# Bilinear FFN behind block-sparse attention: sampled value blocks gathered by GpSimd's indirect DMA, other transfer times in the planner, no parking of products

## Chip, cores and metric

The kernel runs on one core of a Trainium2 chip. The metric is the device time of one execution in microseconds; the time given for a kernel is the median of its runs.

## What is computed

Four batches of eight heads attend over 768 positions of 64 elements, in blocks of 32 positions. The first and the last block attend to everything and are attended by everything, each other block sees its two neighbours and three sampled blocks, which are an input. The result, 3072 rows of 512, goes through a feed-forward layer without a nonlinearity but the product of two projections.

```python
mask = np.abs(blk_i - blk_j) <= window
mask = mask | (blk_i == 0) | (blk_j == 0) | (blk_i == n_blocks - 1) | (blk_j == n_blocks - 1)
for qb in range(n_blocks):
    for kb in sampled_blocks[qb]:
        mask[qb*block:(qb+1)*block, kb*block:(kb+1)*block] = True
...
attn = attn / (np.sum(attn, axis=-1, keepdims=True) + 1e-09)
out = np.matmul(attn, v)                       # then x = out as (B*S, H*D)
a = x @ w_a; b = x @ w_b                       # 512 -> 1536
return a * b @ w_out                           # 1536 -> 512
```

## The kernel before

Work goes by **units**: one query block of 32 positions with all eight heads, 96 in all. Eight units make a **chunk** of 256 positions; there are 12 chunks, three to a batch. Of the 24 units of a batch 22 are sparse (`attend`), the first and the last are dense (`attend_all`).

A sparse unit runs like this. GpSimd (POOL) copies its eight key blocks into `KG`, one of two buffers (`gather_keys`, L573 to L578; the three sampled blocks by addresses that it loads into registers, L553). TensorE (PE) makes the scores `s` (L873, L772), VectorE (DVE) their maximum, ScalarE (ACT) the exponentials `sm`, and the two of them a high and a low half of the weights `hl` (L790 to L797). A transposing DMA on the queue of SyncE (SP) turns `hl` into `pt` (L920). PE multiplies `pt` by the unit's value blocks in `VG` (`av`, L816). `VG` also has two buffers; a unit's eight blocks come from `vd`, the values in DRAM, by DMAs of SP (`gather_values`): the three neighbours in one (L608), the first and last block where the buffer does not hold them yet (L610, L611), and each sampled block by a DMA of its own, whose address SP reads from the table `offs` into a register (L553, L613). A buffer is free when `av` of the unit two before it has run. Two units make a stretch of `xT`, the input of the feed-forward layer (L1060, L1063).

The feed-forward layer runs by chunk and by twelve slices f of the 1536 inner columns: `first_products` makes a and b (`ab`, 24 matmuls, L1098), `inner` multiplies them (L1126, L1129), `split` makes two float32r parts `gh` and `gl` (L1153, L1156), `second_products` multiplies them by `w_out` (`o`, six matmuls, L1184 to L1186). The weights arrive as 64-bit words in 36 loads of 512 KB, and DVE and ACT turn each into the parts that PE reads (L709 to L753); a chunk's slice f waits for `w_ready[f]` in the first chunk. With `PARK` set the second chunk is a flow of its own: `inner` stores its twelve products `a` to DRAM (`parked_g`, L1134), and `unpark` fetches each again (L1147) before it is split.

The order on every engine is fixed at build time by `Plan`. Each step names an engine, a time that it is thought to take and, for a DMA, the time that its bytes hold the DMA engines; the planner issues the step that it thinks can begin first. On the chip every engine works its list off in order, so a step that waits holds whatever stands behind it, on SP's and POOL's queues too. Every DMA of SP and of ACT also takes the next of eight semaphore lanes, and waits until the DMA that had the lane before has landed.

Of the kernel before, what the change touches and what calls it, by code (L numbers as in the profile page):

```python
# [30 lines left out]
LANDING = 1200  # L31
LANES = 8
# [23 lines left out]
PARK = True  # L56
# [69 lines left out]
class Plan:  # L126
# [13 lines left out]
    def begin(self, flow, way):  # L140
# [103 lines left out]
def kernel(  # L244
# [9 lines left out]
    c_blocks: bass.AP,  # L254
    out: bass.AP,
# [69 lines left out]
    offs = const.tile([1, NB, 4], I32, name="offs")  # L325
# [26 lines left out]
    vg_ready = {u: Event() for u in vg_units}  # L352
# [31 lines left out]
    def make_tables():  # L384
# [3 lines left out]
        row = work.tile([P, DM], F32, tag="st", name="mrow", bufs=ST_BUFS)  # L388
# [6 lines left out]
        one = row[0:1, 0 : 2 * NR * NB].bitcast(I32).rearrange("p (a b) -> p a b", b=2)  # L395
        clamped = row[0:1, 256 : 256 + NR * NB]
        clamped3 = clamped.rearrange("p (a b) -> p a b", b=NR)

        def load():
            nc.scalar.dma_start(  # L400
                one.rearrange("p a b -> p (a b)"),
                sampled_blocks.bitcast(I32).rearrange("(o a) b -> o (a b)", o=1),
            )
            nc.scalar.dma_start(
# [6 lines left out]
        def starts():  # L411
            nc.vector.tensor_scalar(
                clamped, one[:, :, 0], 0.0, float(NB - 1), ALU.max, ALU.min
            )
            nc.vector.tensor_scalar(
                offs[:, :, :NR], clamped3, float(BLK), None, ALU.mult
            )
            nc.vector.tensor_scalar(
                offs_k[:, :, :NR], clamped3, float(BLK // 2), None, ALU.mult
            )  # L420

        t = yield dve(700, starts)
# [46 lines left out]
    def keys(b, g):  # L469
        yield from gate(first_of[b] - GATE_KV)  # L470
        raw, freed = yield from raw_tile(b, g, 0)
        yield load_way(1000, lambda: nc.scalar.dma_start(raw, k[b, g]))
# [23 lines left out]
        end = yield sp(1700, 2200, lambda: nc.sync.dma_start_transpose(  # L496
# [6 lines left out]
    def values(b, g):  # L503
# [3 lines left out]
        yield load_way(1000, lambda: nc.scalar.dma_start(raw, v[b, g]))  # L507
# [42 lines left out]
    def dynamic(engine, table, i):  # L550
        eng = {"SP": mybir.EngineType.SP, "POOL": mybir.EngineType.Pool}[engine]
        step, top = (BLK, S - BLK) if table is offs else (BLK // 2, (S - BLK) // 2)
        return nc.values_load_multi_w_load_instructions(  # L553
            table[0:1, i, :NR], engines=(eng,), min_val=0, max_val=top,
# [3 lines left out]
    def gather_keys(n):  # L558
# [13 lines left out]
        def copies():  # L572
# [4 lines left out]
            for r, at in enumerate(dynamic("POOL", offs_k, i)):  # L577
# [8 lines left out]
    def gather_values(n):  # L586
# [10 lines left out]
        def copies():  # L597
# [14 lines left out]
            for r, at in enumerate(dynamic("SP", offs, i)):  # L612
                nc.sync.dma_start(  # L613
                    to[(1 + r) * BLK : (2 + r) * BLK, 1, :], vd[b][bass.ds(at, BLK), :]
                )

        dense = i in (0, NB - 1)
        t = yield [Way("SP", 475 if dense else 3000 + 1250 * first, copies, 1300, 1)]
        vg_ready[b, i, x].fire(t + LATE_VG)

# [6 lines left out]
    def queries(cc):  # L627
# [6 lines left out]
        yield load_way(1400, lambda: nc.scalar.dma_start(t[:D], q[b, c]))  # L634
# [36 lines left out]
    def turn_queries(cc, a):  # L671

        end = yield sp(650, 700, lambda: nc.sync.dma_start(
# [12 lines left out]
    def weights(n):  # L686
# [4 lines left out]
        for m in range(n, n + 1 + both):  # L691
            freed.append((yield from take("w", W_BUFS)))
            yield load_way(1350, lambda m=m: nc.scalar.dma_start(
# [162 lines left out]
    def attend(b, i):  # L856
# [63 lines left out]
        t = yield sp(1300, 1500, lambda: nc.sync.dma_start_transpose(  # L920
# [29 lines left out]
    def attend_quad(b, i, hq, ends):  # L950
# [53 lines left out]
        for x in range(2):  # L1004
# [10 lines left out]
            t = yield sp(1100, 1130, lambda hl=hl, pt=pt: nc.sync.dma_start_transpose(  # L1015
# [56 lines left out]
    parked_g = dram.tile([NF, P, CH], F32, name="parked_g")  # L1072
    g_parked = [Event() for _ in range(NF)]
    split_done = [Event() for _ in range(NF)]
# [4 lines left out]
    def first_products(ccs):  # L1079
        for cc in ccs:  # L1080
# [3 lines left out]
            if cc == 2 and PARK:  # L1084
                yield split_done[NF - 1]
            if cc == 0:
                plan.start(second_products(), R_P2)
            for f in range(NF):
                if cc < 2 and (cc == 0 or PARK):
                    yield w_ready[f]  # L1090
# [19 lines left out]
    def inner(cc, f, ab, read):  # L1110
# [22 lines left out]
        if cc == 1 and PARK:  # L1133
# [157 lines left out]
```

## Time and profile before

| | |
|---|---|
| median of three runs | 901.85 us (900.5 to 905.66) |
| the profiled execution | 901.24 us, of which 899.5 us are the span from the first to the last instruction |
| busy in the span | PE 770.2, DVE 580.0, ACT 464.3, POOL 176.9 us |
| DMA | 145.5 MB; 0.83 to 0.99 of the engines in each 50 us up to 400 us |
| chain that ended last | PE 55%, DMA 14%, DVE 10%, ACT 7%, SP's queue 2% |

PE is busy for most of the span and for nearly all of it after 200 us; before that DVE is. A wait on another engine counts only where one of these two waits in the end.

### The profile page before, as it was taken

How to read it: one execution, taken by the hardware profiler on the slowest of the kernel's cores; microseconds unless marked ns; L12 is line 12 of the kernel's file. 1: busy time of each engine (PE TensorE's matmuls, PEld its weight loads, DVE VectorE, ACT ScalarE, POOL GpSimd, SP SyncE). 2: the span in 40 equal slices, each digit the busy share in tenths (PEclk: the TensorE clock that was granted, in tenths of full speed). 3: DMA queues.
4: the chain of work that ended last, by engine and by line, in shares of the span. 5: the costliest groups of instructions: out<-in, count | busy, mean ns of one | idle time of the engine just before them, and what ended most of it. 6: DMA issues, size and time to landing. Idle time of an engine off the chain costs nothing.

```text
span 899.5 us, 23840 instructions
## 1 busy us (share of the span) xinstructions
PE 770.2 (86%) x9024; PEld 619.3 (69%) x9024; DVE 580.0 (64%) x1533; ACT 464.3 (52%) x1118; POOL 176.9 (20%) x416
## 2 busy tenths in 40 slices
PE   0132499678989999999999899999998999999998
PEld 0022277557768777777777678788776878888886
DVE  3898999986558677665677577645867736342222
ACT  4675576586446566754456468335536424232222
POOL 0652142322003332110132331001322200000000
PEclk9998599899999999999999999999999999999999
DMA  9978999979878699985867999637766516351000
GB/s 228 287 186 218 243 235 252 222 193 206 215 205 181 140 194 210 198 181 136 173 155 170 180 211 206 153 82 159 180 134 155 125 29 153 80 121 27 25 1 24
DMA packets 212221, 145.50 MB, mean 162 GB/s; under 512 B 152841, under 2 KB 180490, under 8 KB 211338
## 3 DMA queue, kind: packets, MB, share of 16 engines
q1 hardware_dynamic: 201280, 106.22, 54.3%
q10 hardware_dynamic: 10826, 37.76, 14.4%
q8 instruction: 71, 1.16, 0.5%
q14 instruction: 44, 0.36, 0.1%
HBM read 87.82 MB, written 14.16 MB: 113 GB/s over the span
## 4 chain that ended last, share of the span: by engine, by line
PE 55%; DMA 14%; DVE 10%; ACT 7%; issue 2%; SPq 2%; ACTq 0%; POOL 0%
PE ab L1098 30%; PE o L1184 6%; PE av L816 5%; DMA pt<-hl 5%; PE o L1186 5%; PE o L1185 5%; DMA q<-in_q_dram 3%; PE s L772 3%; DVE low L888 1%; DVE hl L797 1%; DVE xT L1063 1%; DMA VG<-vd 1%; DVE QT L649 1%; DMA u<-parked_g 1%; ACT sm L898 1%
## 5 line engine op out<-in xcount | busy, mean ns | idle before, releaser
L1098 PE MATMUL ab<-xT,wab 128*128 128x256 f16 x3456 | 404.7, 274 | 12.7 <-ACT xT L1060 6.9
L1098 PEld LDWEIGHTS <-wab 128*128 128x128 f16 x3456 | 329.7, 98 | 78.5 <-issue 37.7
L1129 DVE SCALAR_TENSOR_TENSOR a<-a,rscale,ab 128x256 f32<-128x256 f32 x144 | 68.6, 478 | 112.1 <-ACT a L1126 110.9
L1184 PE MATMUL o<-woh,gh 128*128 128x512 f32 x288 | 127.1, 441 | 6.8 <-ACT gh L1153 6.4
L1126 ACT ACTIVATE a<-ab,f 128x256 f32<-128x256 f32 x144 | 67.5, 468 | 120.3 <-PE ab L1098 114.4
L898 ACT ACTIVATE sm<-s,low,cq 128x256 f32<-128x256 f32 x176 | 97.9, 559 | 58.7 <-DVE low L891 29.4
L816 PE MATMUL av<-pt,VG 128*128 128x64 f16 x2688 | 103.2, 196 | 28.9 <-DMA pt<-hl 14.9
L816 PEld LDWEIGHTS <-VG 128*128 128x128 f16 x2688 | 94.6, 100 | 48.1 <-issue 35.5
L573 POOL COPY KG<-keysT 128x384 int32<-128x384 int32 x88 | 56.9, 647 | 356.5 <-PE s L772 325.9
L797 DVE SCALAR_TENSOR_TENSOR hl<-sm,den,hl 128x256 f16<-128x256 f32 (+1 forms) x208 | 104.3, 510 | 21.4 <-ACT hl L790 18.6
L1186 PE MATMUL o<-woh,gl 128*128 128x512 f32 x288 | 115.2, 400 | 0.5 <-DVE gl L1156 0.5
L1185 PE MATMUL o<-wol,gh 128*128 128x512 f32 x288 | 113.6, 395 | 0.0
L578 POOL COPY KG<-keysT 128x128 int32 x264 | 94.5, 394 | 42.9 <-POOL KG L573 23.2
L1153 ACT CAST gh<-a 128x256 fp32r<-128x256 f32 x132 | 53.1, 403 | 59.2 <-DVE a L1129 58.0
L1156 DVE TENSOR_TENSOR gl<-a,gh 128x256 fp32r<-128x256 f32 x132 | 58.2, 441 | 32.3 <-ACT gh L1153 31.6
L1184 PEld LDWEIGHTS o<-woh,gh 128*128 128x128 f32 x288 | 54.7, 190 | 27.7 <-ACT gh L1153 10.0
L772 PE MATMUL s<-KG,QT 128*32 128x256 f16 x1408 | 58.8, 291 | 16.8 <-DMA QT<-QT 16.6
L873 PE MATMUL s<-mrows,ident 128*32 128x192 bf16 (+1 forms) x352 | 25.6, 280 | 54.7 <-ACT sm L898 27.8
L1063 DVE SCALAR_TENSOR_TENSOR xT<-av,xT 64x256 f16<-64x256 f32 x96 | 40.4, 421 | 44.3 <-ACT xT L1060 43.4
L1186 PEld LDWEIGHTS o<-woh,gl 128*128 128x128 f32 x288 | 54.6, 189 | 16.6 <-DVE gl L1156 4.3
L888 DVE TENSOR_REDUCE low<-s 128x2 f32<-128x512 f32 x88 | 59.9, 682 | 6.4 <-PE s L772 6.1
L772 PEld LDWEIGHTS <-QT 128*32 128x32 f16 x1664 | 43.7, 101 | 29.5 <-issue 24.1
(92 smaller groups left out, 736.0 us busy)
## 6 DMA issues: line engine op xcount, KB each, us to landing
VG<-vd SPq DMA_DIRECT2D x284, 64.0 KB, 2.2
VG<-vd SPq DMA_DIRECT2D x88, 192.0 KB, 3.3
VG<-vd SPq DMA_DIRECT2D x32, 384.0 KB, 3.8
q<-in_q_dram ACTq DMA_DIRECT2D x12, 512.0 KB, 6.0
QT<-QT SPq DMA_DIRECT2D x24, 256.0 KB, 3.8
vd<-vs SPq DMA_DIRECT2D x16, 384.0 KB, 4.1
out_dram<-ou SPq DMA_DIRECT2D x24, 256.0 KB, 2.4
stage<-in_k_dram ACTq DMA_DIRECT2D x12, 384.0 KB, 4.2
```

What stands on the lines that cost most here:

```text
L578: nc.gpsimd.tensor_copy(to[:, :, (5 + r) * w : (6 + r) * w], of[:, :, bass.ds(at, w)])
L772: mm(to[h * BLK : (h + 1) * BLK], q_block(cc, i, 4 * hq + h, a), rhs(4 * hq + h), start=(first and a == 0), stop=(a == 1), skip_group_chec ...
L797: t = yield dve(221 + n * 1.03, lambda: nc.vector.scalar_tensor_tensor(lo, sm, over, hi, ALU.mult, ALU.subtract))
L816: mm(av[:, g, i % 2, :], w, pt[:, y, cols], start=(i % 2 == 0 and g == 0 and first and n + m == 0), stop=(last and n == len(terms) - 1 and ...
L888: yield dve(685, lambda: nc.vector.tensor_reduce(mx, ps, axis=mybir.AxisListType.X, op=ALU.max, negate=True))
L898: t = yield act(750, lambda hq=hq: nc.scalar.activation(sm[:, hq], ps[:, hq], AF.Exp, bias=low[:, at, hq, 0:1], scale=cq[:, cc, hq : hq + ...
L1098: mm(ab[:, i, :], wab[:, f, i, part, kt, :], xc[:, kt, a, :], start=(i == 0 and kt == 0 and part + a == 0), stop=(kt == KT - 1 and a == 1) ...
L1126: yield act(470, lambda: nc.scalar.activation(a_sb, ab[:, 0, :], AF.Copy, scale=fb[:, f : f + 1]))
L1129: t = yield dve(420, lambda: nc.vector.scalar_tensor_tensor(a_sb, a_sb, rb, ab[:, 1, :], ALU.mult, ALU.mult))
L1184: mm(po, gh[:, js], woh[:, f, :], start=(f == 0), stop=False)
L1185: mm(po, gh[:, js], wol[:, f, :], start=False, stop=False)
L1186: mm(po, gl[:, js], woh[:, f, :], start=False, stop=(f == NF - 1))
```

## The change

Three edits go together. (1) The three sampled value blocks of a unit come by one indirect DMA issued from POOL (`gather_sampled`): 96 rows, whose row numbers stand in a new table `taken`, one column per block, made at the start from the sampled blocks broadcast to 96 partitions. SP keeps L608, L610 and L611, and no longer reads addresses; the table `offs` is gone. `vg_ready` of a sparse unit now counts two arrivals. (2) `PARK` and all that hangs on it is gone: the second chunk follows the first in one flow. (3) The planner's times for transfers change (loads of keys and values 1000 to 1340 ns, of queries 1400 to 2200, of weights 1350 to 1590, `pt` 1500 to 1650, and so on), and it knows DMAs from POOL, which it books at 1300 ns on POOL and which take no lane of the eight.

```diff
@@ class Plan
-        if way.moved:
+        if way.moved and way.eng != "POOL":
             at = max(at, self.dma - DMA_AHEAD, self.generator)
...
+        if way.moved and way.eng == "POOL":
+            self.free["POOL"] = at + way.ns
+            self.dma = max(self.dma, at + way.ns + GATHER_LATE) + way.moved
+            flow.ready = self.dma + LANDING
+            return
@@ def make_tables
+            for r in range(NR):
+                ps = slice(r * BLK, (r + 1) * BLK)
+                nc.vector.tensor_scalar(
+                    taken[ps], clamped3[ps, :, r], float(BLK), row[ps], ALU.mult, ALU.add
+                )
@@ def gather_values
-            for r, at in enumerate(dynamic("SP", offs, i)):
-                nc.sync.dma_start(
-                    to[(1 + r) * BLK : (2 + r) * BLK, 1, :], vd[b][bass.ds(at, BLK), :]
-                )
...
+        if not dense:
+            plan.start(gather_sampled(b, i, to), order[b, i] - LEAD_G)
...
+    def gather_sampled(b, i, to):
+        t = yield [Way("POOL", 1300, lambda: nc.gpsimd.indirect_dma_start(
+            to[BLK:, 1, :], None, vd[b], bass.IndirectOffsetOnAxis(ap=taken[:, i : i + 1], axis=0),
+        ), 700)]
+        vg_ready[b, i, 0].fire(t + LATE_VG)
@@ def queries
-        yield load_way(1400, lambda: nc.scalar.dma_start(t[:D], q[b, c]))
+        yield load_way(2200, lambda: nc.scalar.dma_start(t[:D], q[b, c]))
@@ def inner
-        if cc == 1 and PARK:
-            t = yield sp(650, 364, lambda: nc.sync.dma_start(parked_g[f], a_sb))
-            e_a.fire(t)
-            g_parked[f].fire(t)
-            return
         yield from split(cc, f, a_sb, e_a)
-
-    def unpark():
-        for f in range(NF):
-            yield g_parked[f]
...
-            t = yield sp(650, 364, lambda f=f: nc.sync.dma_start(a_sb, parked_g[f]))
-            plan.start(split(1, f, a_sb, e_a), R_NOW, t)
@@ end of the kernel
-            plan.start(first_products([0, *range(2, NC)]), R_P1)
-            plan.start(first_products([1]), R_P1 + 1)
+        plan.start(first_products(), R_P1)
```

SP's list shrinks from 976 rows to 337. This is its piece around the first `pt` transposes of batch 0, before; `pt_466`, `pt_587` and `pt_617` belong to units 1, 2 and 3 of the first chunk, and `VG_85` in the first row to its unit 2.

```order
L608 DMA VG_85<-vd_79 96x1024
L553 TENSOR_LOAD offs
L613 ISA
L613 DMA VG_85<-vd_79 32x1024
L613 ISA
L613 DMA VG_85<-vd_79 32x1024
L613 ISA
L613 DMA VG_85<-vd_79 32x1024
L673 DMA QT_440<-QT_440 64x2048
L920 DMA_TRANSPOSE pt_466<-hl_436 128x8x128
L920 DMA_TRANSPOSE pt_587<-hl_513 128x8x128
L920 DMA_TRANSPOSE pt_617<-hl_517 128x8x128
```

And now, from the values of unit 1 on (`pt_415`, `pt_444`, `pt_523` and `pt_602` are units 0 to 3):

```order
L619 DMA VG_86<-vd_79 96x1024
L621 DMA VG_86<-vd_79 32x1024
L622 DMA VG_86<-vd_79 32x1024
L935 DMA_TRANSPOSE pt_415<-hl_364 128x8x128
L935 DMA_TRANSPOSE pt_444<-hl_409 128x8x128
L935 DMA_TRANSPOSE pt_523<-hl_453 128x8x128
L619 DMA VG_85<-vd_79 96x1024
L935 DMA_TRANSPOSE pt_602<-hl_528 128x8x128
```

Units 1 and 2 are turned ahead of the third unit's values, where all of these stood behind them.

On POOL each gather stands between key gathers. This is a place in batch 1, before, where only key copies follow each other (`KG_83` for one unit, then `KG_84` for the next):

```order
L573 COPY KG_83<-keysT_78 128x8x48
L553 TENSOR_LOAD offs_k
L578 ISA
L578 COPY KG_83<-keysT_78 128x8x16
L578 ISA
L578 COPY KG_83<-keysT_78 128x8x16
L578 ISA
L578 COPY KG_83<-keysT_78 128x8x16
L573 COPY KG_84<-keysT_78 128x8x48
```

And now, in the same stretch; the first row brings values for unit 7 of the batch, the copies under it keys for its unit 13:

```order
L631 DMA VG_85<-vd_80,taken 96x1024
L584 COPY KG_83<-keysT_78 128x8x48
L563 TENSOR_LOAD offs_k
L589 ISA
L589 COPY KG_83<-keysT_78 128x8x16
L589 ISA
L589 COPY KG_83<-keysT_78 128x8x16
L589 ISA
L589 COPY KG_83<-keysT_78 128x8x16
L631 DMA VG_86<-vd_80,taken 96x1024
```

The keys of unit 13 stand behind a row that waits until PE has run `av` of unit 5.

On DVE the start is reordered. Before, the first weights (`wab<-stage`) stand ahead of the low half of the first queries (`QT_140`):

```order
L709 TENSOR_SCALAR wab<-stage 128x1024
L488 SCALAR_TENSOR_TENSOR ks_3_144<-wab,scale,ks_3_144 128x12x64
L713 SCALAR_TENSOR_TENSOR wab<-stage,wab 128x1024
L716 SCALAR_TENSOR_TENSOR wab<-stage,wab 128x1024
L649 SCALAR_TENSOR_TENSOR QT_140<-q_109,scale,QT_140 64x2048
```

Now the queries (`QT_150`) and the tables come first, and the first weights 26 rows after the queries:

```order
L500 SCALAR_TENSOR_TENSOR ks_3_138<-wab,scale,ks_3_138 128x12x64
L381 TENSOR_SCALAR power<-power 128x1
L384 TENSOR_SCALAR rscale<-power 128x1
L387 RECIPROCAL scale<-rscale 128x1
L664 SCALAR_TENSOR_TENSOR QT_150<-q_109,scale,QT_150 64x2048
L554 TENSOR_REDUCE bound<-bound_v 128x1
L422 TENSOR_SCALAR mrow<-mrow 96x72
```

The attention of the first chunk moved ahead of the weights on DVE.

## Rows read from the trace of the kernel before

**Rows 1.** The page's first part: busy time, share of the span and instructions of each engine.

```profile
span 899.5 us, 23840 instructions
PE 770.2 (86%) x9024; PEld 619.3 (69%) x9024; DVE 580.0 (64%) x1533; ACT 464.3 (52%) x1118; POOL 176.9 (20%) x416
```

**Rows 2.** Busy time of each engine in stretches of the span, with the granted clock of TensorE (1.00 is its upper level), the share of the DMA engines and what they moved.

```profile
core 0: us, PE busy (x) PEld busy (x) DVE busy (x) ACT busy (x) POOL busy (x), PEclk, DMA share, GB/s
0.00:50.00 50.00, 5.00 (x80) 3.20 (x80) 31.16 (x84) 27.94 (x52) 19.39 (x37) 1.00 0.93 256
50.00:100.00 50.00, 17.36 (x274) 12.64 (x275) 45.07 (x104) 31.88 (x77) 14.34 (x25) 0.85 0.83 211
100.00:150.00 50.00, 39.65 (x489) 31.73 (x487) 46.42 (x115) 32.55 (x78) 17.15 (x33) 0.88 0.99 236
150.00:200.00 50.00, 36.69 (x440) 28.98 (x437) 46.08 (x118) 34.59 (x82) 13.43 (x24) 0.90 0.84 212
200.00:900.00 700.00, 671.49 (x7754) 542.71 (x7751) 411.22 (x1116) 337.30 (x834) 112.64 (x299) 1.00 0.63 142
```

**Rows 3.** What PE waited for between 200 and 900 us: who and line, whom it waited for: us in total, times, longest us.

```profile
PE o L1184 <- ACT gh L1153: 6.4, 7, 2.4
PE av L816 <- DMA pt<-hl: 5.5, 4, 2.6
PE s L873 <- ACT sm L898: 5.3, 6, 1.8
PE av L816 <- DVE xT L1063: 2.5, 4, 1.0
PE av L816 <- DMA VG<-vd: 0.3, 1, 0.3
```

**Rows 4.** The two longest waits of DVE between 50 and 200 us, same columns.

```profile
DVE hl L797 <- ACT hl L790: 4.2, 2, 3.8
DVE power L374 <- POOL power L371: 1.9, 4, 1.1
```

**Rows 5.** The timeline from 54 to 79 us, SP's queue and the engines that wait at its end: start, us, engine, line, operation, count, and in brackets the idle time before it and what ended that.

```profile
54.27 0.47 DVE L797 SCALAR_TENSOR_TENSOR hl<-sm,den,hl 128x256 f16<-128x256 f32 x1
62.87 0.47 DVE L797 SCALAR_TENSOR_TENSOR hl<-sm,den,hl 128x256 f16<-128x256 f32 x1
...
65.83 0.53 SPq L608 DMA_DIRECT2D VG<-vd  x1
68.14 1.32 SPq L613 DMA_DIRECT2D VG<-vd  x3
...
70.08 7.27 SPq L920 DMA_TRANSPOSE pt<-hl  x3
77.71 0.51 ACT L790 ACTIVATE hl<-sm,den 128x256 f16<-128x256 f32 x1 [5.14 <-DMA pt<-hl]
78.25 0.48 DVE L797 SCALAR_TENSOR_TENSOR hl<-sm,den,hl 128x256 f16<-128x256 f32 x1 [3.78 <-ACT hl L790]
```

**Rows 6.** The chain that ended last, from 257 to 265 us, in order of time (start, us, what), and under it PE's row at 262.35 us in the timeline.

```profile
257.05 0.24 PE o L1184
...
258.55 3.26 DMA u<-parked_g
261.89 0.41 ACT gh L1153
...
263.14 0.43 PE o L1185
...
262.35 0.79 PE L1184 MATMUL o<-woh,gh 128*128 128x512 f32 x1 [2.39 <-ACT gh L1153]
```

**Rows 7.** Instructions of SP's queue by line: count, ns minimum/median/maximum, first and last start.

```profile
L553 SPq TENSOR_LOAD <-offs x88: 666/688/1870, 59.1 to 793.8; - x88
L613 SPq DMA_DIRECT2D VG<-vd x264: 315/316/1436, 60.2 to 795.8; - x132
...
L920 SPq DMA_TRANSPOSE pt<-hl x88: 1237/1284/4338, 53.2 to 774.7; - x88
```

**Rows 8.** POOL: its longest wait over the span; its copies of one sampled key block over the span (ns minimum/median/maximum); the same copies grouped from 50 to 200 us and from 200 to 720 us (busy us, mean ns, idle before them); and one unit's keys in the timeline.

```profile
POOL KG L573 <- PE s L772: 325.9, 61, 55.0
...
L578 POOL COPY KG<-keysT x264: 287/293/2775, 32.6 to 716.6; 128x128 int32 x132
...
L578 POOL COPY KG<-keysT 128x128 int32 x48 | 22.6, 506 | 6.6 <-issue 4.5 <-POOL KG L573 2.1
...
L578 POOL COPY KG<-keysT 128x128 int32 x201 | 62.6, 348 | 35.7 <-POOL KG L573 20.5 <-issue 14.0 <-POOL KG L576 1.0
...
705.66 0.51 POOL L573 COPY KG<-keysT 128x384 int32<-128x384 int32 x1 [6.67 <-PE s L772]
707.55 0.82 POOL L578 COPY KG<-keysT 128x128 int32 x3 [1.39 <-issue]
```

**Rows 9.** DVE's groups by shape over the span: busy us, mean ns of one | idle before.

```profile
L488 DVE SCALAR_TENSOR_TENSOR ks<-stage,scale,ks 128x768 f16<-128x768 f32 x12 | 12.1, 1014 | 1.8 <-ACT ks L487 1.7
L747 DVE SCALAR_TENSOR_TENSOR wab<-wab,scale 128x512 f16<-128x512 f32 x16 | 12.0, 759 | 0.8 <-ACT wab L746 0.7
L888 DVE TENSOR_REDUCE low<-s 128x2 f32<-128x512 f32 x88 | 59.9, 682 | 6.4 <-PE s L772 6.1
```

**Rows 10.** Pieces of the chain that ended last with PE at its upper clock: one sparse unit's scores (two rows), one slice of a first product, one unit's `av`.

```profile
121.02 0.20 PE s L873 x4
121.22 0.47 PE s L772 x16
...
223.66 2.62 PE ab L1098 x24
...
245.84 0.71 PE av L816 x24
```

More of the change, by code (lines that the diff above doesn't have):

```diff
@@ L31 @@
 LANDING = 1200
+GATHER_LATE = 600
 LANES = 8
@@ L324 @@
     mrows = const.tile([P, 8, BLK], BF16, name="mrows")
-    offs = const.tile([1, NB, 4], I32, name="offs")
+    taken = const.tile([NR * BLK, NB], I32, name="taken")
+    row = const.tile([NR * BLK, 1], F32, name="row")
     offs_k = const.tile([1, NB, 4], I32, name="offs_k")
@@ L387, in make_tables @@
         held = yield from take("st", ST_BUFS)
-        row = work.tile([P, DM], F32, tag="st", name="mrow", bufs=ST_BUFS)
+        mrow = work.tile([P, DM], F32, tag="st", name="mrow", bufs=ST_BUFS)
         held2 = yield from take("st", ST_BUFS)
@@ L394, in make_tables @@
         dup = box[:NB, 56:64]
-        one = row[0:1, 0 : 2 * NR * NB].bitcast(I32).rearrange("p (a b) -> p a b", b=2)
-        clamped = row[0:1, 256 : 256 + NR * NB]
+        one = mrow[: NR * BLK, 0 : 2 * NR * NB].bitcast(I32).rearrange("p (a b) -> p a b", b=2)
+        clamped = mrow[: NR * BLK, 256 : 256 + NR * NB]
         clamped3 = clamped.rearrange("p (a b) -> p a b", b=NR)
@@ L547, in values_scale, with dynamic @@
         v_scale[b].fire(end)
-    def dynamic(engine, table, i):
-        eng = {"SP": mybir.EngineType.SP, "POOL": mybir.EngineType.Pool}[engine]
-        step, top = (BLK, S - BLK) if table is offs else (BLK // 2, (S - BLK) // 2)
+    def dynamic(i):
         return nc.values_load_multi_w_load_instructions(
-            table[0:1, i, :NR], engines=(eng,), min_val=0, max_val=top,
+            offs_k[0:1, i, :NR], engines=(mybir.EngineType.Pool,), min_val=0,
+            max_val=(S - BLK) // 2,
             skip_runtime_bounds_check_because="the table is clamped to these bounds",
@@ L576, in copies @@
                 nc.gpsimd.tensor_copy(to[:, :, 4 * w : 5 * w], of[:, :, (NB - 1) * w :])
-            for r, at in enumerate(dynamic("POOL", offs_k, i)):
+            for r, at in enumerate(dynamic(i)):
                 nc.gpsimd.tensor_copy(
@@ L1077, with first_products @@
     f1_ready = {(b, f): Event() for b in range(B) for f in range(NF)}
-    def first_products(ccs):
-        for cc in ccs:
+    def first_products():
+        for cc in range(NC):
             b, c = chunks[cc]
@@ L1088, in first_products @@
             for f in range(NF):
-                if cc < 2 and (cc == 0 or PARK):
+                if cc == 0:
                     yield w_ready[f]
@@ L1132, in inner @@
         read.fire(t)
-        if cc == 1 and PARK:
-            t = yield sp(650, 364, lambda: nc.sync.dma_start(parked_g[f], a_sb))
-            e_a.fire(t)
-            g_parked[f].fire(t)
-            return
-        yield from split(cc, f, a_sb, e_a)
-    def unpark():
-        for f in range(NF):
-            yield g_parked[f]
-            if f >= 2:
-                yield split_done[f - 2]
-            e_a = yield from take("a", A_BUFS)
-            a_sb = work.tile([P, CH], F32, tag="a", name=f"u{f}", bufs=A_BUFS)
-            t = yield sp(650, 364, lambda f=f: nc.sync.dma_start(a_sb, parked_g[f]))
-            plan.start(split(1, f, a_sb, e_a), R_NOW, t)
+        yield from split(cc, f, a_sb, e_a)
     def split(cc, f, a_sb, e_a):
@@ L1166, in second_products @@
             b, c = chunks[cc]
-            if cc == 1 and PARK:
-                plan.start(unpark(), R_NOW)
             rows = out[b * S + c * CH : b * S + (c + 1) * CH, :].rearrange(
@@ L1218 @@
         plan.start(attend(*units[0]), 0)
-        if PARK:
-            plan.start(first_products([0, *range(2, NC)]), R_P1)
-            plan.start(first_products([1]), R_P1 + 1)
-        else:
-            plan.start(first_products(range(NC)), R_P1)
+        plan.start(first_products(), R_P1)
         plan.run()
@@ L1236, in _constants @@
     blocks = np.stack([i - 1, i, i + 1, 0 * i, 0 * i + NB - 1], 1)
-    return [("c_blocks", np.concatenate([blocks, np.eye(NB)], 1).astype(np.float32))]
+    rows = np.arange(96)[:, None] % 32
+    return [
+        ("c_blocks", np.concatenate([blocks, np.eye(NB)], 1).astype(np.float32)),
+        ("c_rows", rows.astype(np.float32)),
+    ]
 def _laid_out(name, a):
```

41 lines of the change are left out of this document (17 added, 24 removed).

## Prediction

> **What bounds the kernel now.** I read the page's busy times first, then the stages, then who waits in each. PE is busy for 770.2 of 899.5 us [rows 1], so 129.3 us of idle PE are all that a change which leaves every matmul in place can win, apart from clock. The stages say where they lie [rows 2]: 45.0 us before 50, 56.3 us from 50 to 200, and 28.5 us in the last 700. From 50 to 200 us DVE is busy for 137.6 of 150 us, and ACT for 99.0: DVE, which unpacks the weights beside the attention of the first units, sets the pace there, and PE idles because its work is not ready; its granted clock of 0.85 to 0.90 there costs little for the same reason. After 200 us PE sets the pace, 671.5 of 700 us. So the kernel is a DVE stage and a PE stage, and I ask of each edit what it does to DVE's waits in the first, and to PE's in the second. The DMA engines are 0.83 to 0.99 busy in the first [rows 2], yet DVE waits little for them.
>
> Of PE's idle time after 200 us the waits with a name are 6.4 us for `gh`, 5.5 for `pt`, 5.3 for the exponentials, 2.5 for `xT`; for `VG` it is 0.3 [rows 3]. So the value blocks themselves are hardly ever late in that stage. What the edit can win lies in what stands behind them on SP.
>
> **SP's queue.** A unit's sampled blocks cost SP one table load and three DMAs: 0.69 + 3 x 0.32 = 1.6 us of instructions, and about 2.7 us from the issue at 65.83 to the start of the first of them plus their own 1.32 [rows 5, 7]; 88 times that is 88 x 1.6 = 141 us at least. It goes. The clearest harm is early. The weights `hl` of unit 1 are done at 54.27 + 0.47 us, those of units 2 and 3 by 62.87 + 0.47, but their transposes begin at 70.08, behind the third unit's values [rows 5]. ACT then waits 5.14 us for the buffer and DVE 3.78 us for ACT. In the new order units 1 and 2 stand ahead of those values. I take the 3.8 us off the DVE stage. The bounds are 0, if the transposes themselves are as late in full DMA engines (7.27 us for three, against 1.28 for the median one [rows 5, 7]), and 4.2 us, all that DVE waits for `hl` there [rows 4].
>
> After 200 us the same relief meets the 5.5 us that PE waits for `pt`. Two waits make up most of it, and I halve it: -2.7, between 0 and -5.5.
>
> **The start and DVE's order.** Before the twelfth product of the first chunk (L1129), after which PE is never short of weights again, DVE's new list holds one residual of keys more (1.01 us), one of weights (0.76), one score maximum (0.68), and some small steps, three of them for the new table: by counting the rows ahead of it and multiplying each by its group's mean [rows 9] I get 194.1 us of work against 191.4, so +2.7. The queries and tables now precede the first weights. That brings the first scores nearer, but the same work stands ahead of the twelfth product either way, so I count nothing, with 4 us to either side for what DVE idles while the tables load. The DVE stage: -3.8 + 2.7 = -1.1.
>
> **Parking.** The 24 transfers and their issues go. Their price on PE is one wait: at 262.35 us PE had idled 2.39 us for a `gh` whose product had come back from DRAM in 3.26 us, and the next six matmuls ran at 0.43 us and more where the hot ones take 0.24 [rows 6], the lower of the two clock levels, about 1.3 us. Together -3.7. The other bound is 0: the second chunk's products now go straight from DVE to PE, and another wait for `gh` may stand there.
>
> **PE's own order.** It changes too, and not for the better. Between the end of a slice's `ab` and its first `o` PE's list must hold enough other work to hide two steps of ACT and two of DVE. Adding up matmuls at the hot durations [rows 6, 10], 16 of 144 slices had under 4 us there, now 27 have. The 4.0 us of `gh` waits left besides parking (6.4 - 2.4) [rows 3], spread over 16, make 0.25 us each, so 11 more cost +2.8; the bounds are 0 and +4.4, at 0.4 us each (6.4 over 16).
>
> **Truer transfer times.** Some of the other named waits, those for exponentials and `xT` (7.8 us) [rows 3], come from loads and transposes that took longer than planned. A quarter less is -2; the bounds are -8 and +2.
>
> **The gather on POOL.** The trace has no indirect DMA. Bounds for what one holds POOL: from below 0.29 us, one copied block [rows 8]; from above 4.3 us, the longest transposing issue on SP [rows 7]. The nearest rows are three plain issues for the same 96 rows, 0.95 us, and the median transposing issue, 1.28 us [rows 7]; I take 1.3. POOL has room for it on the whole: 88 x 1.3 = 114 us more, where it idles 325.9 us waiting for PE to free key buffers [rows 8]. But a gather waits for `av` of the unit two before, and the next keys, and the reductions that scale weights and queries, wait behind it. So it matters how much PE work stands between that `av` and the scores which need those keys. At the place shown it is two scores, two `o` slices and one `av`: 2 x (0.20 + 0.47) + 2 x 6 x 0.24 + 0.71 = 4.9 us [rows 6, 10]. This is the least; fourteen units have under 8, 92 us in sum. One unit's keys take 705.66 to 708.37, 2.7 us [rows 8], and about 0.4 us go to semaphores, an estimate. So up to 1.7 us for a gather nothing happens, and 1.3 is free.
>
> **A gather under DVE's pressure.** The row that warns is the key copy: 0.293 us at the median, 0.506 in the mean from 50 to 200 us, where DVE is busy for 92%, and 2.775 at the worst [rows 8]; so work on POOL stretches 1.7 times there, and 1.2 times later (0.348). A gather of 1.3 us would be 2.2 and then 1.5, which stays free after 200 us. The Trainium skill, "SBUF — State Buffer", section "SBUF: two separate sides", goes further: while VectorE holds the port pair it shares with GpSimd, descriptors of a DMA issued from GpSimd cannot be written, and a transfer of 620 ns became 3100 ns beside a VectorE copy. By its fivefold stretch the gather would be 6.5 us, an estimate from that page, and the sum below would rise by some 40 us. The copies' rows agree on the direction and not on the size.
>
> **Sum.** -1.1 (DVE stage) - 2.7 (`pt`) - 3.7 (parking) + 2.8 (PE's order) - 2 (truer times) = -6.7. The span goes from 899.5 to 892.8. The profiled execution took 901.24, 1.74 more, and the median is 0.6 above that, so the median comes to 895.
>
> **The rivals.** *The waits come back (no change).* The second chunk's products wait for `gh` as before, the tight `ab`-to-`o` gaps cost their 4.4 us, and truer times bring nothing: -1.1 - 2.7 + 4.4 = +0.6, less part of the clock, so 902. For it: PE's waits after 200 us are many and short [rows 3], the mark of a list that always has something tight; against it: the parked wait is one place and is gone.
>
> *POOL becomes the queue that blocks (slower).* With g the length of a gather, a unit loses g + 3.1 minus its lead where that is positive. At g = 4 these losses come to 9 us over the tight units, at g = 5 to 14 x 8.1 - 92 = 21 us, and then the median is 895 + 21 = 916. It outweighs the gains at about g = 3.6. For it: copies stretch on POOL, and four other kinds of work hang on that list. Against it: 1.3 us leaves room even at 1.7 times.
>
> *The relief is larger (much faster).* DVE's waits from 50 to 200 us fall by most of the 6 us named [rows 4] and half of the 28.5 us after 200 goes [rows 2]: -4 + 2.7 - 14 = -15, so 886 and less, to 880.
>
> **How the numbers follow.** Main case 0.42, own range 889 to 897; no change 0.25; POOL blocks 0.18; much faster 0.15. A measurement here can tell about 0.5%, 4.5 us, from no change: under 897.3 is faster, over 906.4 slower. Main and much faster are faster, 0.57; the second is the same, with a little of POOL's mild end, 0.25; 0.18 is slower. The range that leaves out two in ten runs from 881, through the larger relief, to 912, into POOL's case at g of some 4.5 us; the predicted time is the main case's.
>
> **What would show it.** SP's list has no L553 and its transposes begin within 2 to 3 us of their `hl` between 60 and 80 us; DVE's wait of 3.78 us there is gone. No wait for `u`, and PE does not idle 2 us near 260. PE's busy time from 200 us on is over 97% and its idle there 20 to 24 us. The gathers hold POOL for 1 to 2 us, and `s` never waits for `KG`. I am wrong if `s` or DVE waits for POOL by more than 5 us in all, if the DVE stage ends more than 4 us away from 200, or if PE's waits for `gh` after 200 us grow beyond 8 us.

## The result and the profile after

The changed kernel takes 907.93 us (median of 20 runs, 902.54 to 918.85) against 903.25 for the kernel before: ratio 1.0051, interval 1.0029 to 1.0072. It is slower by half a per cent where 0.8 per cent faster was forecast. The profiled execution took 903.19 us, with a span of 901.4. All ratios below are to the kernel before on the same chip; they leave out runs over 1.5% above the fastest of their kernel, so a kernel whose runs scatter can have a median that stands higher than its ratio, and both are given (below, x_G's ratio rests on three of its twelve runs and y_truth's on two of six).

The page after, its busy times, and under it the same stretches as [rows 2] (us of PE, PEld, DVE, ACT and POOL, granted clock, share of the DMA engines, GB/s):

```profile
span 901.4 us, 22960 instructions
PE 775.1 (86%) x9024; PEld 620.7 (69%) x9024; DVE 588.9 (65%) x1544; ACT 461.8 (51%) x1109; POOL 264.7 (29%) x504
...
0.00:50.00 50.00, 5.01 (x80) 3.31 (x81) 28.17 (x77) 26.25 (x49) 13.96 (x30) 1.00 0.84 232
50.00:100.00 50.00, 18.62 (x320) 13.85 (x319) 44.60 (x104) 32.15 (x79) 24.30 (x39) 0.80 0.97 214
100.00:150.00 50.00, 42.23 (x526) 33.08 (x522) 47.93 (x114) 33.30 (x80) 25.61 (x43) 0.93 1.04 256
150.00:200.00 50.00, 31.83 (x300) 23.12 (x301) 44.82 (x121) 32.36 (x72) 18.45 (x24) 0.83 0.78 194
...
200.00:901.40 701.40, 677.36 (x7802) 547.35 (x7801) 423.33 (x1131) 337.71 (x832) 182.35 (x371) 1.00 0.69 139
```

Against [rows 1, 2]: POOL does 88 us more, DVE 9 us. PE idles 45.0 us before 50 as it did, 57.3 from 50 to 200 (56.3), and 24.0 after 200 (28.0 by the same cut at the end). So 3 us of idle time went, and PE's busy time grew by 4.9 for the same matmuls. Part of that is the clock: from 50 to 200 us it was lower in two of the three stretches (0.80, 0.93 and 0.83 against 0.85, 0.88 and 0.90), and it fell once more after 310 us (below).

Where the time went shows best in a running account: time, less the matmul work done by then, every matmul at its duration with the clock at its upper level (24 `ab` 2.62 us, an `o` 0.233, 24 `av` 0.71, as [rows 6, 10]), in us lost so far:

| at us | 120 | 200 | 260 | 280 | 330 | 400 | 500 | 850 |
|---|---|---|---|---|---|---|---|---|
| before | 102 | 122 | 126 | 133 | 134 | 141 | 146 | 165 |
| after | 93 | 125 | 131 | 131 | 140 | 144 | 152 | 169 |
| after, gathers left out (y_none) | 92 | 125 | 131 | 131 | 133 | 137 | 146 | 153 |

After is 9 us ahead at 120 us, 3 behind at 200 and 2 ahead at 280, since before loses 7 us where it unparks its products and after loses none there; then after loses 9 us between 280 and 330. The third line is an experiment, below.

PE's waits after 200 us, as [rows 3], and DVE's longest from 50 to 200, as [rows 4]:

```profile
PE av L831 <- DMA VG<-vd,taken: 5.1, 4, 2.4
PE av L831 <- DVE xT L1078: 3.7, 6, 1.6
PE s L888 <- ACT sm L913: 3.6, 3, 2.1
PE o L1175 <- ACT gh L1148: 3.4, 5, 1.6
PE o L1177 <- DVE gl L1151: 1.5, 2, 1.0
...
DVE power L381 <- POOL power L378: 9.1, 5, 4.5
```

`pt` is gone from the list (5.5 before) and `gh` fell from 6.4 to 3.4; but the values, 0.3 before, now stand first. DVE no longer waits for `hl` (4.2), and waits 9.1 us for POOL's reductions (1.9). This is the place of the 4.5, in timeline rows of POOL, of DVE and, last, of SP:

```profile
50.42 1.09 POOL L631 DMA_INDIRECT VG<-vd,taken  x1 [6.58 <-DVE low L903]
51.82 0.92 POOL L631 DMA_INDIRECT VG<-vd,taken  x1 [0.30 <-issue]
52.75 0.51 POOL L584 COPY KG<-keysT 128x384 int32<-128x384 int32 x1
53.20 0.75 POOL L589 COPY KG<-keysT 128x128 int32 x3
53.94 0.30 POOL L378 PARTITION_ALL_REDUCE power<-bound  x1
...
54.28 0.43 DVE L381 TENSOR_SCALAR power<-power 128x2 int32<-128x2 int32 x1 [4.50 <-POOL power L378]
...
52.39 9.76 SPq L935 DMA_TRANSPOSE pt<-hl  x3
```

The first gather holds POOL's list for 6.58 us, and the reduction for which DVE waits stands behind it. What it waits for is not the DVE row named, but most likely the store of the values that it reads: with a plain DMA in its place (y_plain, below), the trace puts 5.63 us of the same wait down to `vd<-vs`:

```profile
50.55 1.19 POOL L631 DMA_DIRECT2D VG<-vd  x2 [5.63 <-DMA vd<-vs]
```

The three transposes of SP take 9.76 us.

The end of the DVE stage, as the start of the first and the twelfth product on DVE, before (L1129) and after (L1139), and the busy times up to the end of the twelfth:

```profile
118.51 0.48 DVE L1129 SCALAR_TENSOR_TENSOR a<-a,rscale,ab 128x256 f32<-128x256 f32 x1
198.82 0.48 DVE L1129 SCALAR_TENSOR_TENSOR a<-a,rscale,ab 128x256 f32<-128x256 f32 x1
...
0.00:199.30 199.30, 98.06 (x1266) 75.97 (x1267) 168.04 (x418) 126.26 (x283) 64.30 (x117) 0.91 0.90 229
```

```profile
108.69 0.48 DVE L1139 SCALAR_TENSOR_TENSOR a<-a,rscale,ab 128x256 f32<-128x256 f32 x1 [0.61 <-ACT a L1136]
205.47 0.47 DVE L1139 SCALAR_TENSOR_TENSOR a<-a,rscale,ab 128x256 f32<-128x256 f32 x1
...
0.00:205.90 205.90, 102.38 (x1296) 76.77 (x1297) 171.19 (x425) 128.77 (x290) 85.32 (x140) 0.88 0.92 223
```

The first product comes 9.8 us earlier and the twelfth 6.6 us later: DVE is busy 3.2 us longer by then and idle 3.4 us longer (34.7 against 31.3). Of the idle time 3.0 us more lie before 50 us (21.8 against 18.8), ahead of the first gather.

The gathers themselves: their time on POOL (ns minimum/median/maximum), two pieces of the chain that ended last, and PE's rows where two of them were late:

```profile
L631 POOL DMA_INDIRECT VG<-vd,taken x88: 918/948/2441, 50.4 to 796.1; - x88
...
91.96 9.12 DMA VG<-vd,taken
...
301.26 9.73 DMA VG<-vd,taken
...
304.86 0.79 PE L831 MATMUL av<-pt,VG 128*128 128x64 f16 x21 [1.55 <-DMA VG<-vd,taken]
311.04 0.79 PE L831 MATMUL av<-pt,VG 128*128 128x64 f16 x21 [2.35 <-DMA VG<-vd,taken]
```

A gather is short on POOL, 0.95 us, but its data are late. From the packets of its queue in the trace (64 to a gather, in order): the first starts 2.8 us after the gather does, the last ends 4.9 us after it at the median and 10.7 at the worst. Before, a 64 KB value block on SP landed 2.2 us after its issue by the page.

### The profile page after: what moved, and what is told of

It is laid out like the page before. It is cut to its first block, busy times and chain, and to the rows that moved or that the text cites. A ratio compares the mean times of both kernels' runs of the same rounds, so it can differ in the third digit from the quotient of the medians.

```text
span 901.4 us, 22960 instructions
## 1 busy us (share of the span) xinstructions
PE 775.1 (86%) x9024; PEld 620.7 (69%) x9024; DVE 588.9 (65%) x1544; ACT 461.8 (51%) x1109; POOL 264.7 (29%) x504
## 3 DMA queue, kind: packets, MB, share of 16 engines
q0 software_dynamic: 5632, 17.31, 9.1%
## 4 chain that ended last, share of the span: by engine, by line
PE 63%; DVE 14%; DMA 11%; ACT 5%; issue 5%; POOL 2%; POOLq 1%; ACTq 0%; SPq 0%; DVEq 0%
PE ab L1108 34%; PE o L1175 6%; PE av L831 6%; PE o L1177 6%; PE o L1176 5%; PE s L787 4%; DMA VG<-vd,taken 3%; DMA stage<-in_k_dram 2%; DMA pt<-hl 2%; DVE hl L812 2%; DVE xT L1078 1%; DMA keysT<-ks 1%; DVE low L903 1%; PE s L888 1%; DVE QT L664 1%
## 5 line engine op out<-in xcount | busy, mean ns | idle before, releaser
L1108 PE MATMUL ab<-xT,wab 128*128 128x256 f16 x3456 | 409.9, 276 | 11.2 <-ACT wab L761 5.4
L631 POOL DMA_INDIRECT VG<-vd,taken x88 | 93.1, 1058 | 302.9 <-PE av L831 271.8
L1139 DVE SCALAR_TENSOR_TENSOR a<-a,rscale,ab 128x256 f32<-128x256 f32 x144 | 68.7, 477 | 128.5 <-ACT a L1136 127.1
L812 DVE SCALAR_TENSOR_TENSOR hl<-sm,den,hl 128x256 f16<-128x256 f32 (+1 forms) x208 | 107.3, 523 | 3.0 <-ACT hl L805 0.5
L1148 ACT CAST gh<-a 128x256 fp32r<-128x256 f32 x144 | 58.1, 404 | 74.3 <-DVE a L1139 69.2
L1151 DVE TENSOR_TENSOR gl<-a,gh 128x256 fp32r<-128x256 f32 x144 | 64.6, 449 | 30.9 <-ACT gh L1148 29.7
L808 DVE TENSOR_SCALAR hl<-sm,den 128x256 f16<-128x256 f32 (+1 forms) x128 | 47.7, 374 | 31.2 <-DMA pt<-hl 30.6
```

The lines of the kernel that those rows point to most:

```text
L631: t = yield [Way("POOL", 1300, lambda: nc.gpsimd.indirect_dma_start(to[BLK:, 1, :], None, vd[b], bass.IndirectOffsetOnAxis(ap=taken[:, i : ...
L812: t = yield dve(221 + n * 1.03, lambda: nc.vector.scalar_tensor_tensor(lo, sm, over, hi, ALU.mult, ALU.subtract))
L1108: mm(ab[:, i, :], wab[:, f, i, part, kt, :], xc[:, kt, a, :], start=(i == 0 and kt == 0 and part + a == 0), stop=(kt == KT - 1 and a == 1) ...
L1139: t = yield dve(420, lambda: nc.vector.scalar_tensor_tensor(a_sb, a_sb, rb, ab[:, 1, :], ALU.mult, ALU.mult))
```

## The experiments

Theory A: the gather is paid for in waits, of PE for values and of DVE for what stands behind it on POOL, and this eats what the other edits give. Theory B: the order that the planner makes with the new times costs it. Theory C: without parking another wait takes its place.

| run | what | ratio (interval) | median, before's |
|---|---|---|---|
| x_G | edit 1 alone | 1.0027 (0.9978 to 1.0076) | 923.8, 906.2 |
| x_P | edit 2 alone | 0.9967 (0.9926 to 1.0008) | 906.6, 906.2 |
| x_T | edit 3 alone | 1.0061 (1.0025 to 1.0097) | 913.1, 906.2 |
| x_GP | edits 1, 2 | 1.0077 (1.0016 to 1.0139) | 918.0, 908.9 |
| x_PT, x_PT2 | edits 2, 3, timed twice | 0.9894 (0.9853 to 0.9934), 0.9907 (0.9862 to 0.9951) | 898.2, 906.2; 900.4, 909.8 |
| y_none | after, no gathers | 0.9838 (0.9786 to 0.9891) | 890.7, 906.7 |
| y_sp | after, plain DMA on SP | 0.9884 (0.9835 to 0.9933) | 895.1, 906.7 |
| y_plain | after, plain DMA on POOL | 0.9864 (0.9786 to 0.9942) | 895.5, 906.7 |
| y_two | after, two plain DMAs on POOL | 1.0029 (0.9978 to 1.0080) | 906.8, 908.9 |
| z_late0 | after, first gathers later | 0.9994 (0.9941 to 1.0047) | 909.9, 906.7 |
| y_truth | after, gather booked as measured | 1.0143 (0.9978 to 1.0308) | 924.2, 908.9 |
| x_PTj, x_PTk | edits 2, 3, landing 1220, 1180 | 1.0011 (0.9948 to 1.0075), 0.9941 (0.9903 to 0.9978) | 903.2, 908.9; 901.2, 909.8 |
| a_j1, a_j2 | after, landing 1220, 1180 | 1.0013 (0.9970 to 1.0056), 1.0073 (1.0026 to 1.0120) | 910.9, 906.5; 916.3, 906.5 |
| b_j1, b_j2 | before, landing 1220, 1180 | 1.0150 (1.0084 to 1.0216), 1.0001 (0.9959 to 1.0043) | 920.5, 906.5; 908.7, 906.5 |

**The edits one by one.** Each is the diff's part alone; without edit 2, for instance:

```diff
-PARK = True
+PARK = False
```

> The kernel before with edit 1 alone: sampled value blocks by POOL's indirect DMA, old transfer times, parking kept. Theory A (the gather eats the gains: it stands ahead of reductions on POOL and its data land late, 9.1 and 9.7 us in two places of the changed kernel's chain): slower than before by 4 to 12 us, DVE waits for power on POOL by over 5 us between 50 and 200 us, PE waits for VG by over 4 us after 200. Theory B (the new order by the new transfer times puts the weights late): within 3 us of before, and the last weight residual about where it was, at 187 us.

> The kernel before with edit 2 alone: no parking. Theories A and B: faster by 3 to 7 us, since the traces show PE losing 7 us between 260 and 280 us before and none after. Theory C (a wait for gh takes the place of the parked one): within 2 us of before.

> The kernel before with edit 3 alone: the new transfer times, SP's dynamic DMAs and parking kept. Theory A: faster by 0 to 4 us, the term of 2 us of the prediction. Theory B: slower by 5 us or more, with the twelfth product of the first chunk some 6 us later than 199.3 us, as in the changed kernel (205.9).

> The change without edit 1: no parking and the new times, values by SP as before. Theory A: 6 to 11 us faster than before, since the gather's harm is gone and both gains stay. Theory B: 0 to 5 us slower than before, near the changed kernel.

Edits 2 and 3 together, without the gather, are 1 per cent faster than before, and 1.6 per cent faster than the change: A's number, and not B's. Alone, edit 2 gives too little to tell, and edit 3 is slower, by about what B named (5 us or more). Edit 1 is not told from before by the ratio, though its median stands 1.9% above. So the parts do not add up. Why edit 3 alone is slower shows where the parked products come back under the new times (PE's timeline):

```profile
256.46 0.50 PE L1184 MATMUL o<-woh,gh 128*128 128x512 f32 x1 [1.52 <-ACT gh L1153]
259.84 0.50 PE L1184 MATMUL o<-woh,gh 128*128 128x512 f32 x1 [1.73 <-ACT gh L1153]
263.05 0.51 PE L1184 MATMUL o<-woh,gh 128*128 128x512 f32 x1 [1.54 <-ACT gh L1153]
266.71 0.50 PE L1184 MATMUL o<-woh,gh 128*128 128x512 f32 x1 [1.29 <-ACT gh L1153]
```

Four waits, 6.1 us, where [rows 6] has one of 2.39; with edits 2 and 3 PE has none in these 15 us. That is parking's price in these traces, and it speaks against C; the time of edit 2 alone, whose median is before's, does not settle it.

Where edits 2 and 3 gain is not where the prediction looked. Their DVE stage ends 16 us later than before, as the start of the twelfth product shows, and PE catches up after 330 us. The rows are DVE's at that product in x_PT, and PE's busy time from 330 to 850 us before and in x_PT:

```profile
215.13 0.48 DVE L1129 SCALAR_TENSOR_TENSOR a<-a,rscale,ab 128x256 f32<-128x256 f32 x1
...
330.00:850.00 520.00, 502.61 (x5881) 1.00 0.64 142
330.00:850.00 520.00, 512.95 (x6070) 1.00 0.65 146
```

So when that stage ends does not set the time by itself.

**The gather in an unchanged order.** In these runs all numbers of the planner are the changed kernel's, so the order of all other work on every engine stays as it is, and only what stands for a gather differs. The new lines are those of y_none, y_sp, y_plain and y_two, in this order:

```diff
 def gather_sampled(b, i, to):
-    t = yield [Way("POOL", 1300, lambda: nc.gpsimd.indirect_dma_start(
-        to[BLK:, 1, :], None, vd[b], bass.IndirectOffsetOnAxis(ap=taken[:, i : i + 1], axis=0),
-    ), 700)]
+            if vg_order[b, i, 0] < VG_BUFS:
+                nc.gpsimd.indirect_dma_start(
...
+            nc.sync.dma_start(to[BLK:, 1, :], vd[b][0 : NR * BLK, :])
...
+            nc.gpsimd.dma_start(to[BLK:, 1, :], vd[b][0 : NR * BLK, :])
...
+            nc.gpsimd.dma_start(
+                to[BLK + m * 48 : BLK + m * 48 + 48, 1, :], vd[b][m * 48 : m * 48 + 48, :]
+            ) for m in range(2)
```

> The changed kernel with the order of all engines as it is, but only the first gather into each of the two VG buffers is made; the other 86 are left out, so later units read old rows in place of their sampled blocks. Theory A (gathers are paid for in waits: PE for VG, DVE for reductions behind them on POOL): 5 to 12 us faster than the changed kernel, 0.992 to 0.999 of the kernel before. Theory B (the planner's new order is what costs): within 3 us of the changed kernel, 1.002 to 1.008 of before.

> The changed kernel in its own order, but the 96 rows come by one plain DMA of SP at the place where the gather was written, from fixed rows in place of the sampled ones (so the output is of other blocks): same bytes, no indices, SP's queue. Theory A, if it is POOL's queue and the late landing: as fast as without gathers, within 3 us of that run. If the bytes in full DMA engines are what is late: as slow as the changed kernel, 1.003 to 1.008.

> As the run before it, but the plain DMA of 96 fixed rows is issued by POOL, at the same place of the same order. If DMAs issued from POOL are late whatever they carry: near the changed kernel, 1.002 to 1.008 of before, transfers of some 5 us from issue to last packet. If the indices and their rows make it late: near the run on SP, 3 us or more faster than the changed kernel.

> The changed kernel in its own order, the 96 rows by two plain DMAs of POOL with 48 fixed rows each (other blocks than the sampled ones). Together they hold POOL about as long as one gather (2 x 0.51 against 0.95 us), but their data should land as early as those of one plain DMA (3.5 us after the issue, against 4.9 for the gather). If the late landing is the price: within 3 us of the single plain DMA, 0.983 to 0.990 of the kernel before. If the time on POOL is the price: near the changed kernel, 0.998 to 1.008.

Without gathers the changed kernel is 2.1 per cent faster (0.9838 to 1.0051, some 19 us of 908; 13.5 us between the two profiled spans). This is beyond what A expected, and it shows where: the third line of the account above is the same as the second up to 280 us. Until then the 86 gathers left out cost nothing; after it 7 us by 330 and as much again to the end. The first two gathers are made in this run too, so DVE's wait behind them is no part of this. PE in that run from 200 us on, and its waits:

```profile
200.00:887.90 687.90, 672.84 (x7802) 546.47 (x7801) 417.25 (x1134) 337.95 (x832) 121.35 (x300) 1.00 0.56 122
...
PE av L835 <- DVE xT L1082: 3.6, 6, 1.6
PE s L892 <- ACT sm L917: 3.1, 3, 2.1
...
PE av L835 <- DMA VG<-vd: 1.1, 1, 1.1
PE o L1179 <- ACT gh L1152: 1.0, 4, 0.3
```

PE idles 15.1 us there against 24.0: 4.0 less for values, 2.4 less for `gh`, the rest in small pieces. Its busy time is 4.5 us less for the same 7802 instructions. Part of that is again the clock: behind the waits at 304.86 and 311.04 the next 24 `ab` take 4.45 us in the changed kernel, where 2.79 is usual in its timeline, and from 300 to 400 us the granted clock is 0.98 with gathers and 1.00 without.

The plain DMAs of the same 96 rows, from SP or from POOL, are within half a per cent of no gathers at all; the profiled span of the one on POOL is 892.2 us, 9.2 less than with gathers. So neither the bytes nor POOL's queue as such is dear in this order; the indirect form is. One thing goes with the form, and no run here takes it apart: the plain DMAs read the same 96 adjacent rows each time, a gather three blocks that lie apart. One plain DMA on POOL takes

```profile
L631 POOL DMA_DIRECT2D VG<-vd x88: 512/512/703, 50.6 to 786.9; - x88
```

and its last packet ends 3.6 us after its start (6.5 at the worst); the packets are the same in number and size (5632, of them 4224 of 4096 bytes). The indirect one holds POOL 0.44 us longer and its data land 1.3 us later. Two DMAs of half the rows were to tell these two apart and did not: together they hold POOL 1.0 us as planned, but land 4.6 us after the first starts, and not 3.5, in 96 packets to a unit. By the ratio they come out near the gather, 1.0029.

The traces say a little more. PE's waits for `gh` and for values after 200 us with two plain DMAs, and under them what DVE waits for transposes of SP that have to free a buffer of `hl`, from 200 us on with gathers, with two plain DMAs, with one, and without gathers:

```profile
PE o L1175 <- ACT gh L1148: 7.9, 10, 3.1
PE av L831 <- DMA VG<-vd: 0.4, 1, 0.4
...
DVE hl L808 <- DMA pt<-hl: 30.6, 19, 4.1
DVE hl L808 <- DMA pt<-hl: 21.3, 16, 2.6
DVE hl L808 <- DMA pt<-hl: 17.5, 12, 2.7
DVE hl L812 <- DMA pt<-hl: 11.8, 5, 3.2
```

With two plain DMAs PE hardly waits for the values, though they land nearly as late as a gather's; it waits for `gh`, 7.9 us where one plain DMA has 4.0. And DVE's wait for transposes falls in the same order as the four times do. So late transposes on SP may be a third way in which a gather costs; no run tests it, and which price it is stays open.

**The 4.5 us at 54 us.** The first two gathers are held back until the next reduction on POOL has been issued; nothing else moves.

```diff
+        def reduce():
+            nc.gpsimd.partition_all_reduce(
+                power[:, a], bound[:, a], P, bass_isa.ReduceOp.absmax
+            )
+            while held:
+                held.pop(0)()
```

> The changed kernel with one place altered: the first two gathers stand behind the next reduction on POOL (and the key copies ahead of it), all other rows as they were. Theory A: DVE's wait of 4.50 us at 54 us falls under 1 us, and the kernel is 3 to 4.5 us faster than the changed one, 1.000 to 1.002 of before. Rival (DVE has other work late behind it, or weights are not the limit there): within 1.5 us of the changed kernel.

The wait fell, and DVE's next one, not there in the changed kernel, took its place. DVE's rows, and under them SP's:

```profile
61.77 0.15 DVE L388 TENSOR_SCALAR power<-power 128x1 int32<-128x1 int32 x1 [0.67 <-POOL power L381]
67.55 0.48 DVE L822 SCALAR_TENSOR_TENSOR hl<-sm,den,hl 128x256 f16<-128x256 f32 x1 [5.63 <-ACT hl L815]
...
53.38 13.15 SPq L945 DMA_TRANSPOSE pt<-hl  x3
```

ACT waits for a buffer of `hl` until three transposes of SP are through, and these take 13.15 us, 9.76 in the changed kernel. Its account of lost time is at 210 us what the changed kernel's is, 129 us. The ratio is lower by 0.6 per cent, with intervals that overlap, and its median stands above before's. So the trace is the rival's, and the times do not decide.

**The planner told.** The gather booked at 1000 ns and landing 0.6 us later.

```diff
-GATHER_LATE = 600
+GATHER_LATE = 1500
-        t = yield [Way("POOL", 1300,
+        t = yield [Way("POOL", 1000,
```

> The changed kernel with the gather booked as it was measured: 1000 ns on POOL in place of 1300, and landing 0.6 us later in all (3.8 to 4.4 us after the issue). All orders are planned anew. If PE waits because the plan thinks the gather faster than it is: 5 to 10 us faster than the changed kernel, 0.994 to 1.000 of before. If two VG buffers leave the planner no earlier place for a gather: within 4 us of the changed kernel, 1.001 to 1.009.

> Edits 1 and 2 with the old transfer times. If the new times are worth as much beside the gather as without it (the step from edit 2 alone to edits 2 and 3 was 0.7 percent faster): 1.008 to 1.016 of the kernel before. If the new times are what makes the gather dear: 0.994 to 1.001.

Neither helps: 1.0143 with an interval of 1.7 per cent to either side, its median higher still, and 1.0077. Truer numbers for the gather gave no better order, and without the new times edits 1 and 2 are no faster, so these times are not what makes the gather dear.

**How much is the order's luck.** One number of the planner that belongs to no edit is moved by 20 ns, and everything is planned anew:

```diff
-LANDING = 1200
+LANDING = 1220
```

> Edits 2 and 3 again, with one number of the planner moved by 20 ns that stands for no edit (the landing of every transfer, 1200 to 1220 ns), so that all orders are planned anew. If the 1.1 percent that edits 2 and 3 gave are theirs: 0.984 to 0.994 of the kernel before. If a good order fell to them by luck: 0.996 to 1.006.

> Edits 2 and 3 without the gather, with the planner's landing at 1180 ns. With 1200 it was 0.989 of the kernel before, with 1220 it was 1.001. If edits 2 and 3 gain on the whole and 1220 was an unlucky order: 0.986 to 0.996. If 1200 was a lucky one: 0.998 to 1.010.

> The kernel of edits 2 and 3 with nothing else moved, timed once more, since its first comparison rests on six runs. If it is faster than both kernels: 0.986 to 0.994 again. If the first comparison flattered it: over 0.995.

> The changed kernel with the planner's landing of a transfer at 1220 ns in place of 1200, a number that stands for none of the edits; all orders are planned anew. If the 0.5 percent by which the change is slower belong to the edits: 1.002 to 1.009 of the kernel before. If they are of the size by which orders differ by luck: this run and the next lie more than 1 percent apart, or on both sides of 1.

> The same with 1180 ns. Edits: 1.002 to 1.009. Luck of the order: as in the run before it.

> The kernel before with the landing at 1220 ns. If orders differ little: 0.997 to 1.003. If the luck of an order is worth 1 percent, as edits 2 and 3 showed with the same 20 ns: off by 0.5 percent or more.

> The kernel before with the landing at 1180 ns; expectations as for the run before it.

The kernel before becomes 1.5 per cent slower by 20 ns in one direction, and stays as it is in the other. In the slower one PE waits 8.4 us after 200 us for `gh` (6.4 before) and 7.0 us for products of DVE, 6.2 of them at one place:

```profile
210.26 5.26 PE L1098 MATMUL ab<-xT,wab 128*128 128x256 f16 x24 [6.21 <-DVE a L1129]
```

Over three orders each, the kernel before stands at 1.0000, 1.0150 and 1.0001, the changed one at 1.0051, 1.0013 and 1.0073, and edits 2 and 3 at 0.9894 (0.9907), 1.0011 and 0.9941. The half per cent between the two kernels is thus not to be credited to the edits: their means are 1.0050 and 1.0046. Edits 2 and 3 without the gather are the fastest in the mean, some 1 per cent below either (0.9949). But one of their three orders, 1.0011, is no faster than two of before's, and three orders are few where 20 ns move the ratio by 1.2 and 1.5 per cent; that they gain over orders is likely and not shown. Their first order, 898 to 900 us, was timed twice and is faster than both kernels as they stand.

## Why the prediction was wrong

**The gather on POOL is the step that failed**, "1.3 is free". The duration was sized well, 0.95 us at the median where 1.3 was taken, and `s` does not wait for `KG` after 200 us, as forecast. What the step left out is that a gather can cost elsewhere: only POOL's list was asked who waits behind it, and not `av`, which waits for its data. "The value blocks themselves are hardly ever late" was read from SP's blocks, and carried over to a transfer that lands 4.9 us after its start. In the changed kernel's order the gather costs 17 to 19 us by the ratios (y_plain, y_none), each known to some 5 to 7 us, and 9.2 and 13.5 us between the profiled spans, against the 0 in the sum. The waits for values make 4.0 us of this; for most of the rest the traces show where PE lost it, but no run shows why. The rival of POOL had the sign and put a gather of 3.6 us as the point where the change turns slower; it turned with gathers of 0.95.

**DVE's stage** (-1.1 forecast). The count of work ahead of the twelfth product was near: +2.7 forecast, +3.2 busy. The 3.8 us of `hl` went from DVE's waits and came back as the 4.5 us for a reduction behind the first gathers; where those were moved, `hl` was late again, since the transposes were themselves 10 to 13 us for three. The bound of 0 named for that case was the right end. The start, counted as nothing with 4 us to either side, cost 3.0 us more of idle time; it comes with the new times, since DVE idles 21.1 us before 50 us with edit 3 alone too, where before has 18.8. So the stage ends 6.6 us late, beyond the 4 us set as the mark of an error.

**Parking** (-3.7) was right in kind and undersized in place: the account shows 7 us lost from 260 to 280 before, and none after. On the clock edit 2 alone is worth 3 us by the ratio and none by the medians. **`pt`** lost all of its 5.5 us in the changed kernel, twice the -2.7. **PE's own order** (+2.8) is not seen: `gh` fell to 3.4 where it was to grow. **Truer times** (-2) can't be told from the order that they bring: alone 1.0061, beside edit 2 a gain. These four came to -5.6, and with DVE's -1.1 to -6.7, 0.7 per cent; edits 2 and 3 alone gave 0.5 in the mean of three orders and 1.1 in the first. That the sum without the gather is of the same size is luck at least in part: it credits 1.1 us to the end of the DVE stage, which with edits 2 and 3 comes 16 us later, and PE's gain after 330 us stands in no term of that size.

**The stretch by DVE.** The longest gather is 2.44 us, 2.6 times the median, and no plain DMA of POOL is over 0.70 (median 0.51). The fivefold stretch of the Trainium skill, "SBUF — State Buffer", section "SBUF: two separate sides", is not seen on POOL's rows here: the direction agrees for a few gathers (10 of 88 are over 1.2 us), the size does not, and the median stays at 0.95 us. Nor is it seen in when the data land, 10.7 us at the worst being 2.2 times the median. That DVE is what stretches those ten, no run here shows. Whether DVE holds up descriptors after POOL's row has ended, no run here shows.

Of the marks set, SP's list is as forecast; the wait near 260 is gone; PE's idle time after 200 us is 24.0, at the upper end of the 20 to 24 given, at 96.6% busy where over 97% was given. The 2.7 us named for one unit's values on SP do not follow from its rows, which give 2.31 us from 65.83 to 68.14 and 1.32 of their own [rows 5]; no term uses them. DVE waits for POOL by 9.1 us, over the 5 that were named as the sign of an error.

What stays open: whether the 0.44 us on POOL, the 1.3 us of later data, the late transposes or the scattered rows make the gather dear, and how so little comes to 9 to 19 us in 88 units. No run separated these.

## What to carry to other kernels

Do not price a transfer only by how long its queue holds it: ask also when its last packet lands, counted from what releases it, and what else on the DMA engines it makes late. The same bytes by a plain DMA in an unchanged order show at once what an indirect form costs, even where they do not show why. When a planner sets the order, move one of its numbers that means nothing and time the result before a gain or loss of a per cent is credited to an edit: here 20 ns were worth 1.5 per cent. A wait that is taken away ahead of another late thing gives nothing back, so look for what is late next; and the end of an early stage is not the time of the kernel, so check what the later stage makes of it.

## What the runs showed of the hardware

An indirect DMA of 96 rows held POOL for 0.92 to 2.44 us, a plain one of the same bytes for 0.51 to 0.70, and both left the same packets; the data of the indirect one landed 2.7 to 10.7 us after its start (median 4.9), of the plain one 2.3 to 6.5 (median 3.6). Two plain DMAs of half the rows took nearly as long to land as the gather, 4.6 us at the median, in half as many packets again. The transposing DMAs of `pt` took 2.5 and 3.4 times their median early on, 9.76 and 13.15 us for three where one is 1.28 [rows 7]; the share of the DMA engines was 1.04 from 52 to 62 us in the first case and 1.13 from 53 to 67 us in the second.
